# One core, a state-space recurrence and a long convolution: the recurrence taken at every second step, both stages woven into one planned order

## The chip, the cores and the metric

One core of one Trainium2 chip. The metric is the device time of one execution in microseconds (us). A profile is one execution of it, and its span is 1 to 2 us shorter than the time. A run counts as fast, slow or unknown by its clock and by how far it lies above the fastest of the same kernel (over 1.5% is slow); only fast runs are compared.

## The reference, cut to what matters

`x` is 2048 time steps by 1024 features. Two results are mixed by a gate: a diagonal complex recurrence (1024 states) and a causal convolution with filters as long as the sequence.

```python
def _A_ref(x, Lambda_re, Lambda_im, B_re, B_im, C_re, C_im, log_dt, Dskip):
    ...
    Lam_bar = jnp.exp(dt * Lam)
    Bu = jnp.einsum("bld,pd->blp", x + 0j, B_bar)
    for t in range(L):
        h = Lam_bar[None, :] * h + Bu[:, t, :]
        hs.append(h)
    y = 2.0 * jnp.einsum("blp,dp->bld", hseq, Cmat).real + x * Dskip[None, None, :]

def _B_ref(q, k, v, shift_k, ssm_k, ssm_D):
    for t in range(ks):                       # ks = 4
        k_shift = k_shift + k_pad[:, t:t + S, :] * shift_k[:, ks - 1 - t][None, None, :]
    kv = k_shift * v
    ...                                       # FFTs of kv and ssm_k, product, inverse FFT: y
    y = y + kv * ssm_D[None, None, :]
    return q * y

x = A_x
g = _sigmoid((x * gate_w).sum(-1, keepdims=True))
a = _A_ref(x, ...)
b = _B_ref(x, B_k, B_v, B_shift_k, B_ssm_k, B_ssm_D)     # q is x
return g * a + (1 - g) * b
```

## The kernel before

Two stages, one behind the other. The convolution is a Fourier transform in matmuls. It goes in 8 units of 128 channels. Every unit writes its shifted product to DRAM and reads it back in another layout (`kv_scr`), then goes through `stage1`, `spec`, `product`, `inverse`, a shuffle between partitions by DMA (`zb`) and `final`:

```python
def kv_steps(job):
    ...                                       # four taps on DVE
    nc.vector.tensor_tensor(out=acc, in0=acc, in1=vT, op=ALU.mult)
    nc.sync.dma_start(out=kv_scr[c0:c0 + 128, :], in_=acc)
...
for u in range(NU):
    ...
    for q in range(4):
        spec(z, kv, q, 0, "A")
        if u + 1 < NU:
            stage1(a, zs[u + 1], w, 2 * (q % 2), "V")
        spec(z, kv, q, 1, "A")
        pp_new = product(kv)
        ...
        if pend is not None:
            inverse(*pend, "A")
    if u + 2 < NU:
        va[u + 2] = load_A(kv_scr, u + 2, "va")
```

The recurrence turns the complex scan into two real ones: multiply by a rotating phase (tables `tbc`, `tbs`), scan with the real radius, turn back. It does this for each of 4 time blocks of 512 steps and each of 8 state tiles:

```python
for pi in range(NP):
    ...                                       # B.x: 16 matmuls of 512 columns, two copies on ACT
    nc.vector.tensor_tensor(out=t1, in0=tbc, in1=bure, op=ALU.mult)
    nc.vector.tensor_tensor(out=t2, in0=tbs, in1=buim, op=ALU.mult)
    nc.vector.tensor_tensor(out=pre_re, in0=t1, in1=t2, op=ALU.add)
    ...                                       # the same for pre_im
    nc.vector.tensor_tensor_scan(out=Wre, data0=rcol_bc, data1=pre_re, initial=init_re,
                                 op0=ALU.mult, op1=ALU.add)
    nc.vector.tensor_tensor_scan(out=Wim, data0=rcol_bc, data1=pre_im, initial=init_im,
                                 op0=ALU.mult, op1=ALU.add)
    ...                                       # six more DVE operations turn back: hb_re, hb_im
for tl in range(TT_B):
    ...                                       # C.h: 16 matmuls of 512 columns into psy
    nc.scalar.activation(out=ga, in_=psy, func=ACT.Identity, scale=gcols[:, tt_:tt_ + 1])
    nc.scalar.activation(out=m_t, in_=dsk[:, d0:d0 + DHW], func=ACT.Identity, scale=gcols[:, tt_:tt_ + 1])
    nc.scalar.activation(out=pbs, in_=pbb[:, d0:d0 + DHW], func=ACT.Identity, scale=omg[:, tt_:tt_ + 1])
    nc.vector.tensor_tensor(out=u_t, in0=m_t, in1=pbs, op=ALU.add)
    nc.vector.tensor_tensor(out=u_t, in0=u_t, in1=x_tt[:, d0:d0 + DHW], op=ALU.mult)
    nc.vector.tensor_tensor(out=ot[:, d0:d0 + DHW], in0=u_t, in1=ga, op=ALU.add)
```

## Time and profile before

| | before |
|---|---|
| time, median of 4 runs in the rounds with the changed kernel | 644.6 us (644.16 to 646.3) |
| span of the profile | 643.4 us |
| tables and first loads | 0 to 56 us |
| convolution | 56 to 296 us |
| preparation between the stages | 296 to 371 us |
| recurrence and output | 371 to 643 us |

The prediction below shows the lines that carry this table. First a window of the kernel before (stretch in us, its length, then busy us and count of PE, weight loads, DVE, ACT and GpSimd, then granted TensorE clock, share of the DMA engines, GB/s):

```profile
0.00:56.00 56.00, 3.59 (x16) 2.19 (x16) 36.06 (x82) 25.96 (x30) 4.10 (x10) 1.00 1.00 173
```

For its first 56 us PE has next to nothing to do (3.59 us), while the DMA engines are full (1.00). Then two groups and a queue from its page (a group: line, engine, operation, tiles, shapes, count, then busy us and ns of one, then idle before it):

```profile
L573 DVE TENSOR_TENSOR_SCAN Wre<-rv,init_re,pre_re 128x512 bf16<-128x512 f32 x24 | 30.6, 1276 | 0.0
...
L611 ACT ACTIVATE ga<-psy,gcols 128x512 bf16<-128x512 f32 x32 | 21.3, 676 | 38.6 <-PE psy L607 37.5
```

```profile
q1 hardware_dynamic: 157312, 54.54, 39.6%
```

A scan costs DVE 1.28 us and never waits (idle before it 0.0). The first operation of the epilogue stands behind the last output matmul. The main queue keeps the DMA engines busy for 39.6% of the span.

### The profile page before, as it was taken

The page shows a single profiled execution, that of the slowest core. Times are in us where ns is not written, and L with a number is a line of the kernel's source. Part 1 is how long each engine was busy: PE and PEld are TensorE (multiplying, and loading weights), DVE is VectorE, ACT ScalarE, POOL GpSimd, SP SyncE. Part 2 cuts the span into 40 slices and gives each one's busy share as a digit, 9 for nine tenths or more (in the row PEclk, how much of TensorE's full clock was granted, in tenths as well). Part 3 has the DMA queues.
Part 4 walks back from the last instruction along what each step waited for, and adds up shares of the span by engine and source line. Part 5 has one row for each costly group of instructions (what it writes and reads, how often), then busy time and mean ns, then how long its engine had stood idle before and what let it go on. Part 6 is the DMA issues. An engine that isn't in the chain of part 4 may idle for free.

```text
span 643.4 us, 6726 instructions
## 1 busy us (share of the span) xinstructions
PE 410.0 (64%) x2240; PEld 212.4 (33%) x2240; DVE 465.4 (72%) x1059; ACT 306.4 (48%) x415; POOL 4.1 (1%) x10
## 2 busy tenths in 40 slices
PE   0023877484747493953451087999699978998577
PEld 0011654252424362631110033344244433443133
DVE  7649997393939462630372389999999899989952
ACT  3832865454454664741369961264126611552042
POOL 2000000000000000000000000000000000000000
PEclk9999997778887888876875578999889998999579
DMA  9899705564749364135994022041204200110001
GB/s 173 154 163 254 164 26 131 120 143 100 162 84 175 70 131 89 43 98 103 169 201 116 17 83 59 7 131 66 63 4 130 83 0 1 52 64 0 2 16 49
DMA packets 166026, 59.44 MB, mean 92 GB/s; under 512 B 142312, under 2 KB 158696, under 8 KB 165992
## 3 DMA queue, kind: packets, MB, share of 16 engines
q1 hardware_dynamic: 157312, 54.54, 39.6%
q10 hardware_dynamic: 8680, 4.48, 2.8%
q8 instruction: 17, 0.28, 0.2%
q14 instruction: 17, 0.14, 0.1%
HBM read 17.06 MB, written 12.58 MB: 46 GB/s over the span
## 4 chain that ended last, share of the span: by engine, by line
DVE 41%; PE 21%; ACT 11%; DMA 9%; SPq 9%; issue 5%; ACTq 0%; DVEq 0%
DVE Wim L575 5%; DVE Wre L573 5%; DMA va<-kv_scr 4%; SPq L363 4%; PE ps L336 3%; ACT kv L285 3%; PE ps L327 3%; DVE acc L306 2%; PE psy L607 2%; PE psy L604 2%; PE ps L356 2%; SPq L491 2%; DVE pre_re L549 2%; DVE pre_im L555 2%; DVE hb_re L584 1%
## 5 line engine op out<-in xcount | busy, mean ns | idle before, releaser
L285 ACT CAST kv<-ps 128x1024 bf16<-128x1024 f32 x64 | 64.3, 1015 | 65.8 <-PE ps L338 58.3
L283 DVE CAST zkv<-ps 128x1024 bf16<-128x1024 f32 x28 | 34.2, 1220 | 50.0 <-PE ps L327 49.8
L327 PE MATMUL ps<-tab_188,va 128*128 128x256 bf16 x128 | 25.4, 341 | 57.5 <-DMA va<-kv_scr 55.7
L336 PE MATMUL ps<-zkv,fC 128*128 128x512 bf16 x128 | 54.7, 428 | 6.2 <-ACT kv L285 4.9
L604 PEld LDWEIGHTS <-hb_re 128*128 128x128 bf16 x256 | 25.7, 102 | 76.2 <-DVE hb_re L584 46.1
L285 ACT CAST qq<-ps 128x1024 bf16<-128x1024 f32 x32 | 32.5, 1019 | 32.1 <-DMA zb<-qq 29.6
L327 PE MATMUL ps<-tab_188,ka 128*128 128x256 bf16 x128 | 20.9, 295 | 42.0 <-DVE ka L321 41.4
L285 ACT CAST zkv<-ps 128x1024 bf16<-128x1024 f32 x36 | 36.1, 1022 | 22.1 <-PE ps L327 22.0
L607 PEld LDWEIGHTS <-hb_im 128*128 128x128 bf16 x256 | 26.1, 103 | 47.6 <-issue 18.4
L542 ACT ACTIVATE bure<-bu_re 128x512 bf16<-128x512 f32 x32 | 19.1, 597 | 47.3 <-PE bu_re L535 18.5
L613 ACT ACTIVATE m_t<-dsk,gcols 128x512 bf16<-128x512 bf16 x32 | 23.1, 723 | 35.6 <-DVE u_t L617 32.7
L611 ACT ACTIVATE ga<-psy,gcols 128x512 bf16<-128x512 f32 x32 | 21.3, 676 | 38.6 <-PE psy L607 37.5
L337 PE MATMUL ps<-zkv,fS 128*128 128x256 bf16 x128 | 38.4, 300 | 0.0
L338 PE MATMUL ps<-zkv,fN 128*128 128x256 bf16 x128 | 38.3, 299 | 0.0
L356 PE MATMUL ps<-pp,gC 128*128 128x256 bf16 x128 | 32.5, 288 | 8.6 <-ACT kv L285 5.0
L327 PEld LDWEIGHTS <-va 128*128 128x128 bf16 x128 | 14.9, 120 | 64.2 <-DMA va<-kv_scr 57.5
L374 PE MATMUL ps<-zb,tabFc 128*128 128x512 bf16 x32 | 15.1, 473 | 28.7 <-DMA zb<-qq 28.7
L573 DVE TENSOR_TENSOR_SCAN Wre<-rv,init_re,pre_re 128x512 bf16<-128x512 f32 x24 | 30.6, 1276 | 0.0
L575 DVE TENSOR_TENSOR_SCAN Wim<-rv,init_im,pre_im 128x512 bf16<-128x512 f32 x24 | 30.5, 1271 | 0.0
L543 ACT ACTIVATE buim<-bu_im 128x512 bf16<-128x512 f32 x32 | 19.1, 596 | 22.5 <-PE bu_im L538 22.5
L306 DVE TENSOR_TENSOR acc<-acc,tmpj 128x2047 bf16<-128x2047 bf16 (+2 forms) x24 | 29.3, 1222 | 0.5
L357 PE MATMUL ps<-pp,gN 128*128 128x128 bf16 x128 | 29.2, 228 | 0.0
(793 smaller groups left out, 1153.3 us busy)
## 6 DMA issues: line engine op xcount, KB each, us to landing
zb<-qq SPq DMA_DIRECT2D x128, 64.0 KB
ka<-in_B_ssm_k_dram SPq DMA_DIRECT2D x8, 512.0 KB
kv_scr<-acc SPq DMA_DIRECT2D x8, 512.0 KB
va<-kv_scr SPq DMA_DIRECT2D x8, 512.0 KB
pB_scr<-cv SPq DMA_DIRECT2D x16, 256.0 KB
out_dram<-ot SPq DMA_DIRECT2D x16, 256.0 KB
pbb<-pB_scr ACTq DMA_DIRECT2D x8, 256.0 KB
x_tt<-in_A_x_dram SPq DMA_DIRECT2D x8, 256.0 KB
```

Source lines behind the costliest of these rows:

```text
L283: nc.vector.tensor_copy(o, i_)
L285: nc.scalar.copy(o, i_)
L306: nc.vector.tensor_tensor(out=acc[:, j:S], in0=acc[:, j:S], in1=tmpj[:, 0:S - j], op=ALU.add)
L327: nc.tensor.matmul(ps[:, i, :], lhsT=a[:, 4 * q + i, :], rhs=t1v, start=True, stop=True)
L336: nc.tensor.matmul(ps[:, i], lhsT=fC[:, k2, :], rhs=z[:, k2], start=True, stop=False)
L337: nc.tensor.matmul(ps[:, i, :, 0, :], lhsT=fS[:, k2, :], rhs=z[:, k2, :, 1, :], start=False, stop=False)
L338: nc.tensor.matmul(ps[:, i, :, 1, :], lhsT=fN[:, k2, :], rhs=z[:, k2, :, 0, :], start=False, stop=True)
L356: nc.tensor.matmul(ps[:, i], lhsT=gC[:, k2, :], rhs=pp[:, i], start=True, stop=False)
L573: nc.vector.tensor_tensor_scan(out=Wre, data0=rcol_bc, data1=pre_re, initial=init_re, op0=ALU.mult, op1=ALU.add)
L575: nc.vector.tensor_tensor_scan(out=Wim, data0=rcol_bc, data1=pre_im, initial=init_im, op0=ALU.mult, op1=ALU.add)
L604: nc.tensor.matmul(psy, lhsT=hb_re[:, pi, tl * 128:(tl + 1) * 128], rhs=CTr[pi][:, d0:d0 + DHW], start=(cnt == 0), stop=(cnt == n_mm - 1))
L607: nc.tensor.matmul(psy, lhsT=hb_im[:, pi, tl * 128:(tl + 1) * 128], rhs=CTi[pi][:, d0:d0 + DHW], start=(cnt == 0), stop=(cnt == n_mm - 1))
```

## The change

**Intent.** (1) Let the scan run over even time steps only, and get the odd states from the even ones by diagonal matmuls on PE, so that DVE has half as many blocks. (2) Take the recurrence over all time, state tile by state tile. The output then needs all states at once, so half of them are spilled to DRAM and read back. (3) Spread the convolution units among the recurrence. (4) No pools and no dependence-driven scheduling: the builder lists every operation with an assumed duration and a priority, simulates the core and thereby fixes the order on each engine and the place of each buffer (21 slabs of 8 KB, 8 PSUM halves). (5) Smaller matters: fused epilogue, gates in four column strips of the array, some transfers issued from GpSimd, warm-up matmuls at the start.

The diff has some 1700 lines; this is its core, with cuts marked.

```diff
+class _Plan:
+    def op(self, eng, dur, fn, r=(), w=(), prio=0.0, dma=None, alt=None):
+        ...                                # records what it reads and writes
+    def schedule(self, free0):
+        ...                                # simulates: the ready operation of least priority number goes next
+                        cand = sorted((o for o in waiting[e] if o.ready <= now + 1e-9), key=lambda o: (o.prio, o.idx))
+                        ...
+                        if not take(o):    # no slab or PSUM half free
+                            continue
...
-                nc.vector.tensor_tensor(out=t1, in0=tbc, in1=bure, op=ALU.mult)
-                nc.vector.tensor_tensor(out=t2, in0=tbs, in1=buim, op=ALU.mult)
-                nc.vector.tensor_tensor(out=pre_re, in0=t1, in1=t2, op=ALU.add)
-                ...
+            def turn(out, x):
+                TT(out=out, in0=tab.ap.unsqueeze(2).to_broadcast([128, 2, 2, CW]),
+                   in1=x.unsqueeze(1).to_broadcast([128, 2, 2, CW]), op=ALU.mult)
+            def f():
+                turn(T.ap, ue())
+                TT(out=T.ap[:, 0, 0, :], in0=T.ap[:, 0, 0, :], in1=T.ap[:, 1, 1, :], op=ALU.add)
+                TT(out=T.ap[:, 0, 1, :], in0=T.ap[:, 0, 1, :], in1=T.ap[:, 1, 0, :], op=ALU.subtract)
+            op("DVE", 2.08, f, r=[(H, 0), tab], w=[T], prio=pr)
...
+        def odd(dg, Hc, pi, c, pr):
+            def f():
+                for ri in range(2):
+                    PE_.matmul(ps.ap[:, ri, :], lhsT=ident, rhs=Hc[c].ap[:, 1, ri, :], start=True, stop=False)
+                    for k in range(2):
+                        PE_.matmul(ps.ap[:, ri, :], lhsT=dg.ap[:, LMAT[ri][k], :], rhs=Hc[c].ap[:, 0, k, :],
+                                   start=False, stop=(k == 1))
+            op("PE", 6 * MM(512), f, r=[dg, Hc[c]], w=[ps], prio=pr)
+            evac(lambda: Hc[c].ap[:, 1], lambda: ps.ap, r=[ps], w=[(Hc[c], 1)], prio=pr)
+            if pi < NP - NKEEP:
+                dma(QB, 1.6, lambda: [h_scr[pi, c]], lambda: [Hc[c].ap.rearrange("p a b s -> p (a b s)")], [Hc[c]],
+                    [(e_h, (pi, c))], pr, alt=QA)
...
-                    nc.scalar.activation(out=ga, in_=psy, func=ACT.Identity, scale=gcols[:, tt_:tt_ + 1])
-                    ...
-                    nc.vector.tensor_tensor(out=ot[:, d0:d0 + DHW], in0=u_t, in1=ga, op=ALU.add)
+                op("DVE", 0.77, lambda: STT(out=ot.ap[:, ti, :], in0=ps.ap, scalar=col(gcols, gi[ti]),
+                                            in1=pb.ap[:, ti, :], op0=ALU.mult, op1=ALU.add),
+                   r=[ps, pb, e_gate], w=[(ot, ti)], prio=prs[ti])
...
+    sg = s5()
+    next(sg)
+    conv()
+    for _ in sg:
+        pass
+    order = pl.schedule({"DVE": 9.8, "ACT": 9.5, "PE": 4.6, "POOL": 3.0, "SP": 0.7})
+    with tc.manual_schedule():
+        pl.emit(order, slabs, psums)
```

## The prediction

> **What bounds the kernel now.** I read the page first, for the shape of the span in time:
>
> ```profile
> span 643.4 us, 6726 instructions
> PE 410.0 (64%) x2240; PEld 212.4 (33%) x2240; DVE 465.4 (72%) x1059; ACT 306.4 (48%) x415; POOL 4.1 (1%) x10
> ...
> PE   0023877484747493953451087999699978998577
> ...
> DVE  7649997393939462630372389999999899989952
> ...
> PEclk9999997778887888876875578999889998999579
> ```
>
> No engine is at its limit over the whole span, but the digits show two kernels one behind the other. In slices 1 to 18 (the convolution, 16 us a slice) PE and DVE take turns; in slices 24 to 38 (the recurrence) DVE stands at 8 and 9. Then the windows view with one window per stage (columns: busy us and count of PE, weight loads, DVE, ACT, POOL, then granted clock, DMA share, GB/s):
>
> ```profile
> 56.00:296.00 240.00, 152.51 (x1064) 102.47 (x1064) 153.82 (x249) 130.80 (x135) 0.00 (x0) 0.84 0.54 115
> 296.00:371.00 75.00, 23.20 (x76) 8.28 (x77) 28.26 (x60) 49.06 (x60) 0.00 (x0) 0.64 0.62 122
> 371.00:644.00 273.00, 230.70 (x1084) 99.47 (x1083) 247.28 (x669) 100.52 (x191) 0.00 (x0) 0.91 0.15 48
> ```
>
> Convolution: 240 us in which PE and DVE each have 153 us of work, so neither bounds it and about 87 us are waiting. Between the stages: 75 us where no engine is busy two thirds of the time, because tables, C and x are made ready only then. Recurrence: DVE busy 247 of 273 us, it is the bound there. The waits view says what is waited for in the convolution:
>
> ```profile
> ACT kv L285 <- PE ps L338: 58.3, 34, 7.2
> PEld L327 <- DMA va<-kv_scr: 57.5, 6, 13.5
> PE ps L327 <- DMA va<-kv_scr: 55.7, 6, 13.1
> DVE zkv L283 <- PE ps L327: 49.8, 11, 10.8
> ```
>
> The first stage of a unit stands behind a DRAM round trip (55.7 us in six waits); a single unit is in work, so nothing fills the hole. The chain of waits, in a part of the recurrence, shows DVE following itself:
>
> ```profile
> 432.02 1.19 DVE Wre L573
> 433.40 0.33 DVE r_t_3549 L582
> 433.73 1.19 DVE Wim L575
> 434.93 0.32 DVE ot L619
> ```
>
> A 128x512 product costs the chain 0.33 us and a scan 1.19 us (their recorded spans are 0.42 and 1.27: neighbours overlap). And the timeline gives the price of a matmul when nothing holds it up:
>
> ```profile
> 420.11 0.38 PE L607 MATMUL psy<-CiT_2588,hb_im 128*128 128x512 bf16 x1
> ...
> 420.32 0.38 PE L604 MATMUL psy<-CrT_2600,hb_re 128*128 128x512 bf16 x1
> ...
> 420.54 0.38 PE L607 MATMUL psy<-CiT_2602,hb_im 128*128 128x512 bf16 x1
> ```
>
> 0.215 us start to start, though each record lasts 0.38. At half clock it is 0.43 (the records at 310 us).
>
> **What the Trainium skill says.** "TensorE: Matmul & The Clock Gate", section "Wait — 56ns, not 53.3ns?": warm, back-to-back matmuls start N/2.4 ns + about 2.5 ns apart, 215.7 ns for 512 columns and 55.6 for 128. The trace agrees: 0.215 above, and 71.79 to 71.85 us for a 128-column one. Same page, "What's actually happening": after an idle window of about 3.4 us the clock falls to half and needs as long to recover. The granted clock of 0.84 and 0.64 where PE starves and 0.91 where it is dense fits. "VectorE: DVE Perf Modes", "Side-by-side: where the cycles go for N=2048 bf16": a two-source bf16 operation of 2048 elements takes 1224 ns; the trace has 1.22 us (acc on L306). "SBUF — State Buffer", "Who interferes with whom": a DVE instruction in a two-port mode and GpSimd exclude one another, and DMAs issued from GpSimd need that port for their descriptors. The kernel before issues none there, so its trace can't say.
>
> **The change part by part.**
>
> 1. *Recurrence decimated by two.* The scan runs over even time steps only; odd states come from even ones by a complex multiply with a diagonal, done as matmuls. Before, each of 32 blocks (8 state tiles x 4 time blocks) had 12 products or sums and 2 scans: 12 x 0.34 + 2 x 1.2 = 6.5 us, plus tiny carries, 0.9 us: 236 us. After, 16 blocks of 512 even steps, each with two 128x2048 products with a broadcast operand (1.2 each), four 128x512 sums (0.34) and two scans (1.2): 6.2 us, in all 99. DVE saves about 137 us. PE pays: 64 matmuls of 511 columns for the previous odd input (13.8 us) and 96 of 512 for the odd states (20.7), 34 us more.
> 2. *Epilogue.* Before, 3 sums on DVE and 3 ACT operations for each of 32 half tiles: 39 and 67 us. After, one fused DVE operation from PSUM (22 us; 0.7 us each is my estimate, a little over half of the 1.22 us of a 1024-wide PSUM read on DVE), 30 fused ones (21) and 15 products (10) ahead of it: 53 us on DVE, but only the 0.7 us lies behind the matmuls. ACT keeps 32 x 0.71 = 23.
> 3. *Convolution.* The same columns on PE: stage 1 now 512 matmuls of 128 columns, 28.6 us; spectrum 55.6; inverse 28.3; final 13.8. DVE: shift taps 61, products 32 x 1.2 + 64 x 0.34 = 60 (before 0.6 + 4 x 0.34 for each of 32, about 63), the final multiply by x moves into the PSUM read (16 x 1.22 = 20). Of the 28 + 8 evictions DVE had, 10 stay; ACT has 197 x 1.02 = 201 us of them.
> 4. *All else*: C scaling 18 us and tables 26 on DVE.
>
> Sums from the changed kernel's order of instructions and these prices: DVE 362 us by recorded spans (about 345 start to start), before 465. ACT 289, before 306. PE: B·x 110.6, previous 13.8, odd 20.7, convolution 126.3, output 110.5, gates 2 to 7 (four column strips, perhaps side by side), warm-up 6: 391 to 396 us with the array warm. For the kernel before the same sum is about 350. So PE becomes the engine with most work, and the whole question is how densely it is fed.
>
> 5. *Interleaving and a planned order.* This is the greatest part: it removes the two-kernels shape. The 87 us of holes, the 75 us between, and the recurrence's 42 us of idle PE (273 less 231) have other work to fill them. PE's order shows it: up to 277 us of its own work, B·x, odd states and convolution alternate every few microseconds; then output; the last 368 output matmuls (79 us) are one unbroken run.
> 6. *Added traffic*: spilled states 8 x 0.5 MB written and read, and x once more for the convolution's product, 16 x 0.25 MB: 12.4 MB on 59.4.
>
> **The end, from two sides.** PE side: the gates need all of x. Ahead of it lie about 5 MB of transposing loads; before, five of 0.5 MB issued from 34.1 to 47.4 us, 2.66 us each, so 10 x 2.66 + 3 = 30 us. By then PE can have done 18 us of real work. 384 (without warm-up) - 18 = 366 us remain: 396 us. From the last matmul to the end of the span took 4.5 us before: floor 400. DVE side: its first rotation needs x whole and one B·x more, about 40 us; 283 us of DVE work lie between it and the last rotation, 269 start to start: 309; odd matmul and eviction 3; behind the last odd state PE has 91.5 us of output left, and 4.5 of tail: 408. Both engines must be nearly perfect to meet at 400 to 408. I add 4% for the granted clock (0.93 to 0.98 in the dense windows from 400 to 600 us) and 4% for waits that a fixed order can't dodge, 15 us each: **430 us**.
>
> **The rivals.**
> - *DMA becomes the bound.* Before, 42.4% of 643 us is 273 us of all 16 engines. With 71.8 MB at the same efficiency it is 330 us, 77% of 430. For it: slices at 9 at the start, packets under 512 B are 142312 of 166026, and transposes queue on one in-order issuer. Against it: the added spill is in 4 KB rows, and it spreads over the whole span. If it bites, loads land late and a fixed order can't work around them: 455 to 490.
> - *GpSimd-issued transfers starve.* 84 of the 128 shuffles of the inverse go there, four per group, while DVE's taps run in a two-port mode. Those take about 23 us of DVE time in all, so I expect delays of under 1 us, with nine buffers to hide them: 0 to 15 us.
> - *Broadcast operands lose the fast DVE mode.* The innermost 512 stay contiguous, so I expect 1.2 us; at one element a cycle 63 instructions would take about 1.07 us more each: 67 us, DVE the bound, about 490.
> - *The plan holds.* If PE stays warm and order fits, 405 to 412.
> - *Serialisation eats all*, as an in-order issue queue did before (the shuffles' queue waited 95.5 us for ACT). Even if PE had only today's 64% density, 391/0.64 = 611: still faster.
>
> **Range and chances.** The floors put the low end at 408; DMA or order trouble of the size named puts the high end at 465. Slower would need a density below today's, so faster by over 2%: 0.97, within 2%: 0.02, slower: 0.01.
>
> **What would show it.** Right: PE busy over 85% of the span from 30 us, granted clock 0.93 or more, DVE busy near 360, ACT near 290, 128x2048 products at 1.2 us, no DVE idle of tens of microseconds. Wrong: PE idle released by DMA in total above 40 us (rival one), DMAs from GpSimd with long waits on DVE (rival two), L911 or L772 near 2.3 us (rival three), clock under 0.88 (my 4% too small), PE idle released by DVE (DVE is the bound, the sum of part 4 too small).

## The result, and the profile after

The changed kernel takes 430.31 us (median of 4 runs, 428.82 to 435.28; one of them slow) against 644.6. The ratio of the fast runs is 0.6667 (95% interval 0.6649 to 0.6685). Here and below, a ratio is the mean time of one kernel's fast runs over the mean of the other's of the same rounds, so it is not quite the ratio of the medians. The outputs agree with the reference.

The page of the changed kernel, the lines that answer to those of the kernel before:

```profile
span 427.0 us, 7194 instructions
...
PE 398.4 (93%) x2691; PEld 228.5 (54%) x2736; DVE 346.7 (81%) x513; ACT 267.8 (63%) x310; POOL 132.7 (31%) x172
...
PE   7598999999999789999969999899989999999996
...
DVE  4998999999979789989889989979696969724422
...
PEclk9999999999999999999998999999999999999999
...
q1 hardware_dynamic: 146120, 54.55, 69.8%
q0 software_dynamic: 7360, 16.85, 16.9%
```

The two-kernels shape is gone. PE stands at 9 in nearly all slices, DVE mostly at 8 and 9 in the first 25, and the clock at full. The DMA engines went from 42.4% to 87% of the span (69.8 and 16.9 and small change): 71.87 MB (before 59.44) now move in two thirds of the time.

Where 216.4 us of span went, in PE's own terms. The full-clock price of PE's instructions (the sum in the prediction) was about 350 us before and is about 391 after, both worked out from 0.215 us per 512 columns. What PE was busy beyond that (half clock, drains) fell from 60 us (410.0 less 350) to 7 (398.4 less 391). What it was idle fell from 233 us (643.4 less 410.0) to 29 (427.0 less 398.4). So: 41 us more work, 53 us less lost to the clock, 205 us less idle.

The windows of the changed kernel, cut where the gates can start and where the last odd state is made:

```profile
0.00:37.00 37.00, 28.26 (x219) 18.50 (x222) 31.00 (x74) 22.48 (x31) 32.55 (x28) 0.95 1.12 148
37.00:331.00 294.00, 278.65 (x2056) 168.67 (x2091) 262.96 (x360) 219.58 (x244) 100.11 (x144) 0.99 0.97 184
331.00:427.00 96.00, 91.53 (x417) 41.37 (x423) 52.78 (x80) 25.77 (x36) 0.00 (x0) 0.99 0.49 127
```

In the 294 us of the middle PE lacks 15.35 us, DVE 31 and ACT 74, and the DMA engines are at 0.97. No engine but PE is near its limit. Whether the transfers are is not shown by their share of 0.97: the share passes 1 in the first window (1.12), and nopoolq below moves the same 184 GB/s in this stretch at a share of 0.90. The end is output alone. Why the cut lies at 331, the view of the odd states' line says (first and last start at the end of the times):

```profile
L950 PE MATMUL ps<-slab,slab x62: 377/379/380, 54.4 to 330.9; 128*128 128x512 bf16 x62
```

From the last of these matmuls to the end are 96.1 us, which the prediction put at 91.5 and 4.5. The chain of waits of the changed kernel (start, us, what):

```profile
13.16 6.07 SPq L513
...
29.68 7.28 DMA slab<-in_A_x_dram
37.00 1.91 PE ps L964 x31
...
55.62 6.91 PE ps L882 x32
...
68.14 0.89 PE ps L747 x16
...
212.17 11.65 DMA slab<-in_B_ssm_k_dram
...
353.05 10.74 PE ps L1125 x49
```

One piece of x holds the issuing queue (SPq) for 6.07 us, the last is issued at 29.68 us and lands 7.28 us later; then the gates' 31 recorded matmuls take 1.91 us (32 of 512 columns one behind the other would be 6.9: the four strips run side by side). 32 matmuls of 512 columns in 6.91 us are 0.216 us each and 16 of 128 columns in 0.89 us are 0.056, full speed. From 343.94 us the chain is output matmuls alone. What PE waits for in the middle stretch, from the waits view of that window (us in total, times, longest):

```profile
PE ps L747 <- POOL slab L712: 6.2, 2, 3.5
PE ps L786 <- DVE slab L776: 1.7, 2, 1.4
PE ps L805 <- DMA slab<-slab: 1.6, 1, 1.6
```

L712 is a small addition on GpSimd to a filter tile just loaded (0.69 us in the worst place), and the chain shows the load ahead of it: 512 KB that took 11.65 us from issue to landing. So the longest hole of PE is a transfer with a GpSimd operation behind it. The rest is crumbs. Last, three groups whose duration the prediction guessed:

```profile
L1134 DVE SCALAR_TENSOR_TENSOR slab<-ps,gcols,slab 128x512 bf16<-128x512 f32 x32 | 23.6, 747 | 39.1 <-PE ps L1125 36.1
...
L911 DVE TENSOR_TENSOR slab<-slab,slab 128x2048 bf16<-128x2048 bf16 x31 | 37.7, 1217 | 3.5 <-PE ps L747 1.5
L772 DVE TENSOR_TENSOR slab<-slab 128x2048 bf16<-128x2048 bf16 x32 | 38.6, 1215 | 1.8 <-ACT slab L520 1.5
```

The broadcast products (L911, L772) take 1.22 us, the fused operation from PSUM (L1134) 0.75.

### The profile page after: what moved, and what is told of

Same layout as the page of the kernel before. It is cut to its first block, busy times and chain, and to the rows that moved or that the text cites. A ratio compares the mean times of both kernels' runs of the same rounds, so it can differ in the third digit from the quotient of the medians.

```text
span 427.0 us, 7194 instructions
## 1 busy us (share of the span) xinstructions
PE 398.4 (93%) x2691; PEld 228.5 (54%) x2736; DVE 346.7 (81%) x513; ACT 267.8 (63%) x310; POOL 132.7 (31%) x172
## 2 busy tenths in 40 slices
DMA packets 153596, 71.87 MB, mean 168 GB/s; under 512 B 129861, under 2 KB 147541, under 8 KB 153561
## 3 DMA queue, kind: packets, MB, share of 16 engines
q1 hardware_dynamic: 146120, 54.55, 69.8%
q0 software_dynamic: 7360, 16.85, 16.9%
HBM read 24.93 MB, written 16.79 MB: 98 GB/s over the span
## 4 chain that ended last, share of the span: by engine, by line
PE 68%; DMA 11%; SPq 10%; ACT 4%; DVE 3%; issue 3%; POOL 0%; DVEq 0%; ACTq 0%; POOLq 0%
PE ps L1125 22%; PE ps L882 20%; SPq L513 8%; DMA slab<-slab 5%; PE ps L760 4%; ACT slab L520 4%; PE ps L747 4%; DMA slab<-in_A_x_dram 4%; PE ps L889 3%; PE ps L950 3%; DMA slab<-in_B_ssm_k_dram 3%; PE ps L761 2%; PE ps L786 2%; PE ps L762 2%; SPq L515 2%
## 5 line engine op out<-in xcount | busy, mean ns | idle before, releaser
L520 ACT CAST slab<-ps 128x1024 bf16<-128x1024 f32 x197 | 185.4, 1042 | 62.8 <-PE ps L892 17.6
L882 PE MATMUL ps<-slab,slab 128*128 128x512 bf16 (+1 forms) x527 | 115.8, 370 | 6.3 <-DMA slab<-in_A_B_re_dram 3.1
L1125 PE MATMUL ps<-slab,slab 128*128 128x512 bf16 x485 | 109.1, 379 | 1.0 <-DVE slab L1134 0.4
L882 PEld LDWEIGHTS <-slab 128*128 128x128 bf16 x544 | 52.8, 99 | 60.0 <-issue 5.5
L1125 PEld LDWEIGHTS <-slab 128*128 128x128 bf16 x512 | 49.8, 98 | 59.6 <-issue 0.7
L515 POOL DMA_DIRECT2D slab<-slab x84 | 51.4, 618 | 57.8 <-ACT slab L520 51.9
L1134 DVE SCALAR_TENSOR_TENSOR slab<-ps,gcols,slab 128x512 bf16<-128x512 f32 x32 | 23.6, 747 | 39.1 <-PE ps L1125 36.1
L760 PE MATMUL ps<-slab,fC 128*128 128x512 bf16 x118 | 44.9, 381 | 1.1 <-ACT slab L520 0.6
L747 PE MATMUL ps<-tab,slab 128*128 128x128 bf16 x512 | 35.0, 222 | 7.5 <-POOL slab L712 6.2
L911 DVE TENSOR_TENSOR slab<-slab,slab 128x2048 bf16<-128x2048 bf16 x31 | 37.7, 1217 | 3.5 <-PE ps L747 1.5
L772 DVE TENSOR_TENSOR slab<-slab 128x2048 bf16<-128x2048 bf16 x32 | 38.6, 1215 | 1.8 <-ACT slab L520 1.5
L747 PEld LDWEIGHTS <-slab 128*128 128x128 bf16 x512 | 31.4, 99 | 12.3 <-POOL slab L712 6.8
L761 PE MATMUL ps<-slab,fS 128*128 128x256 bf16 x128 | 35.0, 273 | 0.6 <-issue 0.2
```

The source lines that it names most:

```text
L515: QS[q].dma_start(out=o_, in_=i_)
L520: op("ACT", 1.04, lambda: A.copy(o_(), i_()), r=r, w=w, prio=prio, alt=("DVE", 1.2, lambda: V.tensor_copy(o_(), i_())))
L747: PE_.matmul(ps.ap[:, i, :], lhsT=a.ap[:, 8 * q + i, :], rhs=t1v[:, hh * 128:(hh + 1) * 128], start=True, stop=True)
L760: PE_.matmul(ps.ap[:, i], lhsT=fC[:, k2, :], rhs=zz, start=True, stop=False)
L761: PE_.matmul(ps.ap[:, i, :, 0, :], lhsT=fS[:, k2, :], rhs=zz[:, :, 1, :], start=False, stop=False)
L772: TT(out=T.ap, in0=K.unsqueeze(2).to_broadcast([128, 2, 2, 4 * CH]), in1=W_.unsqueeze(1).to_broadcast([128, 2, 2, 4 * CH]), op=ALU.mult)
```

## The experiments

The prediction came true, so the question is whether for its reasons. The letters in the expectations stand for theories. A: the amount of PE work ahead of the last odd state sets the time. B: the fixed order with its small waits sets it, and every engine has slack that swallows part of any addition. C: transfers are at their limit. D: the second issuer, GpSimd, is needed. E: it is the searched order that brings PE to 93%. G: the gain is the two stages lying beside each other; G': it is the lighter DVE work. In dve18 and act17, B means that the loaded engine is itself a second bound, as the expectations say.

Twelve kernels ran: the first eight below on one chip, the last four on another. Each was compared with the kernel before on the same chip (medians 644.05 to 644.35). All twelve outputs passed the comparison with the reference; experiment 2 shows how little that vouches for.

### 1. pe20: 20 us more PE work, same order

```diff
                 for ri in range(2):
+                    for _ in range(3):
+                        PE_.matmul(ps.ap[:, ri, :], lhsT=ident, rhs=Hc[c].ap[:, 1, ri, :], start=True, stop=True)
                     PE_.matmul(ps.ap[:, ri, :], lhsT=ident, rhs=Hc[c].ap[:, 1, ri, :], start=True, stop=False)
```

> Same plan (order and buffers) as the changed kernel; each odd-state step issues its two identity matmuls of 512 columns three times more: 96 matmuls x 0.2158 = 20.7 us more on PE, result unchanged. Theory A (PE's work sets the time, 93% busy): +18 to +22 us, so about 449 to 453 against 430.3. Theory B (the engines wait on each other in turn and PE's density is incidental): less than half of it, +3 to +10 us, because part falls into PE's idle 28.6 us.

Measured: 443.12 us (442.45 to 445.4), ratio 0.6883 (0.6859 to 0.6907). Against the changed kernel (0.6667, and 0.6686 in a later control) that is 12.7 to 13.9 us. The busy line of this run's page and the line of its odd states:

```profile
PE 417.8 (95%) x2786; PEld 237.6 (54%) x2832; DVE 346.9 (79%) x513; ACT 268.4 (61%) x310; POOL 134.4 (31%) x172
```

```profile
L952 PE MATMUL ps<-slab,slab x61: 379/379/380, 53.8 to 345.0; 128*128 128x512 bf16 x61
```

PE has 19.4 us more, the last odd state comes 14.1 us later (345.0 against 330.9), and the tail behind it is the same (440.6 less 345.0 = 95.6). PE's idle time fell from 28.6 to 22.8: some 6 us went into holes. About 0.65 us per us of PE work: between the two theories, in the range of neither.

### 2. noident: 6.9 us less PE work, same order

This kernel leaves a term out and is mathematically wrong; the comparison does not see it at its tolerance, so that passing it vouches little for the recurrence, in the changed kernel too.

```diff
-                    PE_.matmul(ps.ap[:, ri, :], lhsT=ident, rhs=Hc[c].ap[:, 1, ri, :], start=True, stop=False)
                     for k in range(2):
                         PE_.matmul(ps.ap[:, ri, :], lhsT=dg.ap[:, LMAT[ri][k], :], rhs=Hc[c].ap[:, 0, k, :],
-                                   start=False, stop=(k == 1))
+                                   start=(k == 0), stop=(k == 1))
```

> Wrong result on purpose: the same plan with the identity matmuls left out (32 x 0.2158 = 6.9 us less on PE), nothing in their place. Theory A: -5 to -7 us, 423 to 425. Theory B: within 1.5 us of 430, the others' waits move into the hole.

Measured: fast runs 427.34, 429.08 and 431.41, ratio 0.6662 (0.6628 to 0.6695): no gain that could be told from none against 0.6667, about 1.5 us against the control. One run was slow (447.0) and the profile fell on it, so no trace of a fast run is at hand. Theory A misses here, B holds. Taking PE work away in this order buys little. That what PE waits for does not come sooner would explain it, but without a fast trace it is not shown.

### 3. dve18: 18 us more DVE work, same order

```diff
                 turn(U.ap, W.ap)
+                turn(U.ap, W.ap)
```

> Same plan; the second 128x2048 product of every rotation is done twice: 16 x 1.15 to 1.22 = 18.4 to 19.5 us more on DVE, result unchanged. Theory A: DVE (81% busy) has slack, but up to 300 us it is 90% busy and feeds PE, so +4 to +10 us. Theory B (DVE is a second bound up to the last rotation, as my floor of 408 us said): +14 to +19 us.

Measured: 433.87 us (430.95 to 434.19), ratio 0.6723 (0.6696 to 0.675): 2.4 to 3.6 us more.

```profile
PE 397.3 (93%) x2691; PEld 227.3 (53%) x2736; DVE 364.6 (85%) x529; ACT 268.4 (63%) x310; POOL 147.0 (34%) x172
```

This page shows DVE with 17.9 us more. About a fifth of that or less reaches the end, though all of it lies on the way to a state; the control's interval (0.6653 to 0.6718) even overlaps. That is less than either theory expected. DVE is not the bound.

### 4. act17: 17 us more ACT work, same order

Each odd state is copied out of PSUM twice.

```diff
-            evac(lambda: Hc[c].ap[:, 1], lambda: ps.ap, r=[ps], w=[(Hc[c], 1)], prio=pr)
+            op("ACT", 1.04, lambda: (A.copy(Hc[c].ap[:, 1], ps.ap), A.copy(Hc[c].ap[:, 1], ps.ap)), r=[ps], w=[(Hc[c], 1)], prio=pr,
+               alt=("DVE", 1.2, lambda: (V.tensor_copy(Hc[c].ap[:, 1], ps.ap), V.tensor_copy(Hc[c].ap[:, 1], ps.ap))))
```

> Same plan; the eviction of every odd state is done twice: 16 x 1.04 = 16.6 us more on ACT (a few on DVE), result unchanged. Theory A: ACT is 63% busy, +1 to +5 us, from the added latency only. Theory B: +8 to +16 us.

Measured: fast runs 432.04, 433.33 and 437.13, ratio 0.6738 (0.6697 to 0.6779): 3.4 to 4.6 us more (a fourth run, 440.09, was slow, and the profile fell on it). About a quarter of the addition, as theory A expected; here too the control's interval overlaps. ACT is not the bound either.

### 5. spill2: the spilled states written twice

```diff
+    h_scr2 = dram.tile([NP, NC, 128, 4 * CW], BF16, name="h_scr2")
...
-                dma(QB, 1.6, lambda: [h_scr[pi, c]], lambda: [Hc[c].ap.rearrange("p a b s -> p (a b s)")], [Hc[c]],
+                dma(QB, 1.6, lambda: [h_scr[pi, c], h_scr2[pi, c]], lambda: [Hc[c].ap.rearrange("p a b s -> p (a b s)")] * 2, [Hc[c]],
```

> Same plan; each of the eight spilled state blocks is written to DRAM twice: 8 x 0.5 MB = 4.2 MB more on 71.9 MB, 8 more issues, result unchanged. The queues' shares of the changed kernel's page add up to 87%, so 4.2 MB is about 22 us of all 16 engines. Theory C (transfers are a second bound, since the chain of waits goes through an 11.65 us filter load at 212 us and 69 us of other queue and DMA pieces): +8 to +20 us. Theory A (PE alone): +0 to +3 us.

Measured: 434.33, 441.13, 454.18 and 457.15 us. Only the first counts as fast, so there is no ratio: the size is inconclusive. The one fast run, the profiled one, is 4 us above the changed kernel's median.

```profile
HBM read 24.93 MB, written 20.98 MB: 106 GB/s over the span
```

This line of its page confirms the 4.2 MB (16.79 MB written without). The other three runs count as slow, and noident, which adds no transfer, also had a run 20 us above its fastest; so the spread can't be put down to the added transfers. Whether transfers are near their limit stays open here.

### 6. nopoolq: every transfer issued from one queue

Same order, same buffers; the transfers planned for GpSimd are issued by SyncE.

```diff
-    QS = {"SP": nc.sync, "POOL": nc.gpsimd}
+    QS = {"SP": nc.sync, "POOL": nc.sync}
```

> Same order of instructions; every transfer that GpSimd issues (84 shuffles and 33 others) is issued from the SP queue at its place in that order. Rival two of the prediction (transfers issued on GpSimd starve beside VectorE): faster by 3 to 12 us. Theory D (the second issuer is needed[...]): slower by 20 to 80 us.

Measured: 427.75 us (426.26 to 428.2), ratio 0.663 (0.6609 to 0.6652): 2.4 us faster than the changed kernel and 3.6 than the control, though the intervals just touch the changed kernel's. Theory D is refuted.

```profile
PE 401.0 (94%) x2691; PEld 229.0 (54%) x2736; DVE 345.6 (81%) x513; ACT 267.7 (63%) x310; POOL 62.2 (15%) x57
```

```profile
37.00:331.00 294.00, 282.15 (x2054) 169.91 (x2082) 265.96 (x366) 221.04 (x247) 32.73 (x32) 0.98 0.90 184
```

GpSimd's recorded time falls from 132.7 to 62.2 us; no other engine's busy time changes by more than 2.6. The middle stretch moves the same 184 GB/s at a share of 0.90 instead of 0.97. The Trainium skill, "DMA: Bandwidth & Descriptors", section "Issuing engines are not separate DMA queues", says that issuing on several engines only saves issue time, since the same 16 DMA engines do the work; this run agrees. For the prediction's GpSimd rival it gives a net figure: 2.4 to 3.6 us. A larger loss could hide only behind an equal cost of the single queue, which no run separates.

### 7. nowarm: 2 warm-up matmuls in place of 70

```diff
-            for _ in range(16):
+            for _ in range(1):
                 for j in range(2):
                     PE_.matmul(wps.ap[64 * j:64 * j + 64, 0, 0:128], ...)
-            for _ in range(6):
+            for _ in range(0):
...                                           (the two other groups likewise)
```

> Same plan; the 70 warm-up matmuls ahead of the first real one are cut to 2. If the granted clock of the first real matmuls depends on them: [...]PE waits for loads there in any case, so +0 to +2 us; the granted clock of the first 20 us falls from 0.98 to below 0.9.

Measured: 426.68 us (424.0 to 427.18), ratio 0.6613 (0.6588 to 0.6639): about 0.8% faster than the changed kernel. Its first window:

```profile
0.00:20.00 20.00, 14.08 (x92) 10.22 (x94) 14.46 (x45) 7.09 (x13) 16.44 (x20) 1.00 1.03 161
```

The column of the granted clock reads 1.00 in the first 20 us, not below 0.9 as I expected (from 20 to 40 us it was 0.91, against 0.93 with the warm-up). But that column does not show how the array starts. The first matmuls of B.x do, here and then in the changed kernel (ns least/median/most, first and last start):

```profile
L882 PE MATMUL ps<-slab,slab x32: 272/394/417, 9.1 to 14.3; 128*128 128x256 bf16 x32
L882 PE MATMUL ps<-slab,slab x32: 269/273/273, 10.0 to 15.7; 128*128 128x256 bf16 x32
```

Without the warm-up their median is 394 ns, with it 273. So the warm-up did speed them up; but PE then waited 2.1 and 3.1 us for loads all the same (two waits of L882 in the changed kernel), and the kernel without it was no slower. Why it was even 3.5 us faster is not shown.

### 8. order474: the same operations in a worse order

Only the priorities differ, shifted at random by a few units. The builder's own model takes this order for 47 us longer.

```diff
     PX = [95.0, 1.8]
+    PS = [[-423.74, -1082.05, 23.98, -789.47, -202.9, -1089.84, -331.87, -507.96, 64.56, -211.94, -1260.01], ...
...                                           (all other tables likewise; this row was -427.2, -1083.5, 24.9, -780.9 and so on)
```

> The same work (same matmuls, same transfers), with the priorities of the plan shifted at random by a few units; the builder lays out another order, which it believes to be 47 us longer. Theory E (the fixed order carries a large part of the gain): 465 to 485 us, PE busy the same 398 us, idle 70 us or more. Theory F (the engines' queues and semaphores smooth such differences out): 430 to 445 us.

Measured: 465.48 us (464.34 to 470.7), ratio 0.7239 (0.7196 to 0.7283): 36 us slower. Its windows and the longest waits of PE from 300 to 370 us:

```profile
0.00:300.00 300.00, 272.43 (x2037) 166.57 (x2071) 265.33 (x386) 221.66 (x250) 123.25 (x155) 0.98 1.01 177
300.00:370.00 70.00, 41.78 (x224) 22.20 (x225) 40.89 (x64) 34.03 (x43) 3.56 (x4) 0.76 0.66 135
370.00:468.00 98.00, 94.54 (x435) 42.99 (x441) 41.69 (x60) 14.67 (x22) 0.00 (x0) 1.00 0.30 94
```

```profile
PE ps L1132 <- DVE slab L1072: 12.3, 1, 12.3
PE ps L812 <- DMA slab<-in_A_x_dram: 8.1, 1, 8.1
PE ps L793 <- DVE slab L783: 6.4, 3, 4.7
```

Up to 300 us PE is nearly as dense as in the changed kernel (272.43 us busy against 277.60). Then come several holes. Output matmuls wait 12.3 us for a C tile that DVE has not scaled yet; DVE itself had waited 9.4 us for the load of that C, which was issued late. The last matmuls of the convolution wait 8.1 us, put down to a load of x, and 6.4 for DVE. The clock falls to 0.76, and 28 of 70 us are idle. Over the span PE is idle for 60.2 us (28.6 in the changed kernel) and busy for 408.7, where I expected 70 or more and the same 398. The busy time of DVE and ACT is the same to 3 us. So the order by itself is worth tens of us, and most of them are lost in a few late tiles near the end, not in a general thinning. Theory E holds.

### 9. seq: the same operations, convolution first

Added dependences keep the recurrence's loads, tables and B.x behind the last or last but one convolution unit, and the priorities were searched anew. The search had fewer tries than the author's, so the time may be a little too long. The load of the filter taps moves to the start of the kernel here and in experiment 10, since in the planned kernel three of the four taps declare no dependence on it; the original order meets it by its timing.

```diff
-                op("PE", 2 * ND * MM(CW), lambda: part(0, CW), r=[BT, (t, 0), (t, 1)], w=[ps], prio=pr)
+                op("PE", 2 * ND * MM(CW), lambda: part(0, CW), r=[(e_pB, (u, h)) for u in range(NU) for h in range(2)] + [BT, (t, 0), (t, 1)], w=[ps], prio=pr)
...                                           (likewise on the loads of B, x, C and the tables)
     sg = s5()
...                                           (conv() called ahead of it)
```

> Undoes the interleaving alone: the same operations as the changed kernel (decimated recurrence, fused epilogue), but B and x are loaded, the tables made and the recurrence's matmuls started only when the convolution has all but ended; its order is planned by the same builder with priorities of mine, searched for less long than the original's, so it is an upper bound of what that structure needs. Theory G (the interleaving carries most of the gain): 500 to 540 us, PE busy about 398 again and idle about 110. Theory H (the lighter work carries it): 430 to 460 us. The filter coefficients' tiny load is moved to the prologue here and in the next run, for a dependence that the original's plan meets by luck.

Measured: 516.58 us (514.83 to 521.76), ratio 0.8029 (0.7988 to 0.8069). The windows of this run and, from its timeline, the first matmul of the recurrence:

```profile
0.00:240.00 240.00, 160.61 (x1446) 119.23 (x1447) 171.11 (x263) 178.19 (x194) 52.16 (x78) 0.84 0.91 160
240.00:300.00 60.00, 50.18 (x282) 24.91 (x281) 34.69 (x58) 31.82 (x42) 6.18 (x8) 0.92 0.89 177
300.00:420.00 120.00, 120.00 (x584) 54.91 (x583) 98.33 (x132) 46.36 (x51) 17.03 (x27) 1.00 0.39 110
420.00:516.00 96.00, 92.12 (x427) 41.57 (x425) 45.09 (x70) 22.43 (x31) 0.00 (x0) 1.00 0.37 99
```

```profile
246.80 3.44 PE L890 MATMUL ps<-slab,slab 128*128 128x512 bf16 x8 [5.54 <-DMA slab<-in_A_B_re_dram]
```

By stages, against the kernel before: the convolution with all that precedes it ends at 241 us (before: 296), so 55 us less. PE then waits 5.5 us for B (before: 75 us of preparation, some of which, such as the scaling of C, now lies in the last stage), 70 us less. From there to the end are 269.5 us (516.3 less 246.8; before: 273). **In sequence the decimated recurrence is hardly shorter than the old one**: PE has 120.00 us of 120 between 300 and 420, so PE has taken DVE's place as the bound there, at nearly the same length. And the convolution alone leaves 79 us of PE holes in 240, at a clock of 0.84, with the transfers at 0.91. PE is busy for 422.9 us in all, not the 398 I expected, and idle for 93. Woven together (430) the kernel is 84 to 88 us faster than this (84 by the medians of the same chip, 87 to 88 by the ratios). Theory G expected this time; but 128 us come without any interleaving.

### 10. dve2: rotations and scans done twice, planned so

The interleaved order, with DVE's work of the recurrence doubled, as if it had not been decimated, and planned with those durations.

```diff
-            op("DVE", 2.08, f, r=[(H, 0), tab], w=[T], prio=pr)
+            op("DVE", 4.16, lambda: (f(), f()), r=[(H, 0), tab], w=[T], prio=pr)
...
-            op("DVE", 2.5, g, r=[T] + ([wl] if c else []), w=[W], prio=pr)
+            op("DVE", 5.0, lambda: (g(), g()), r=[T] + ([wl] if c else []), w=[W], prio=pr)
...
-            op("DVE", 2.08, h, r=[W, tab], w=[U, (H, 0)], prio=pr)
+            op("DVE", 4.16, lambda: (h(), h()), r=[W, tab], w=[U, (H, 0)], prio=pr)
...                                           (new priority tables; the taps' load as in experiment 9)
```

> Undoes the saving of the decimation on DVE alone: every rotation and scan is done twice (the same values again), planned with doubled durations: about 98 us more on DVE, near the price of the undecimated recurrence, while PE keeps its work. Theory G': with the convolution spread among it, DVE becomes the bound: 345 + 98 = 443 start to start before the last rotation's 97 us tail is counted, so 495 to 520 us. Theory H' (interleaving alone would do): 430 to 450.

Measured: 495.41 us (491.85 to 500.55, the last one slow), ratio 0.7671 (0.7647 to 0.7695).

```profile
PE 422.2 (86%) x2736; PEld 234.4 (47%) x2736; DVE 417.6 (85%) x600; ACT 332.3 (67%) x353; POOL 65.1 (13%) x75
```

This page has DVE at 417.6 (some copies went over to ACT, 332.3). DVE is busy for 340.7 of the 363.0 us up to the last odd state, and 130.5 us follow (96.1 in the changed kernel). The interleaved plan with all other changes, but without the lighter DVE work, is 149 us faster than the kernel before; the lighter DVE work then gives 63 to 65 more. That is an upper value, since the priorities were searched anew here too. The fourth kernel of this square, in sequence with the doubled DVE work, was not run.

### 11 and 12. best and after_ctl: a better version, and a control

`best` joins nopoolq and nowarm. `after_ctl` is the changed kernel with a comment added, as a control on the same chip.

```diff
-    QS = {"SP": nc.sync, "POOL": nc.gpsimd}
+    QS = {"SP": nc.sync, "POOL": nc.sync}
...
-            for _ in range(16):
+            for _ in range(1):
```

> The changed kernel with two parts taken out, same order otherwise: no warm-up matmuls (70 cut to 2) and no transfers issued from GpSimd. Each alone measured 2.5 to 3.6 us better. If both are real and independent: 422 to 425 us; if they were the luck of a chip or of one alignment of transfers: 426 to 430, same as the control.

> Control: the changed kernel unaltered (a comment added), on the same chip as the other three: 428 to 432 us, ratio 0.665 to 0.669.

Measured: best 426.5 us (425.07 to 428.51), ratio 0.6622 (0.6604 to 0.664). Control 432.69 us (427.08 to 437.88, six runs, one slow), ratio 0.6686 (0.6653 to 0.6718). The intervals just miss each other: the two edits together give about 1%, not more than either alone, in part by having no late runs (all four within 3.5 us).

```profile
PE 400.0 (94%) x2668; PEld 226.5 (54%) x2668; DVE 345.6 (82%) x513; ACT 267.2 (63%) x310; POOL 60.5 (14%) x57
```

PE is at 400.0 of a 423.3 us span. This version beats the changed kernel by a little.

## Why the prediction was right, and where its steps were not

**The number.** 430.0 was predicted and 430.3 measured, but not by the terms of the sum alone; errors cancelled. In the trace of the changed kernel PE's account reads: gates ready at 37.0 us; behind that 370.2 us of PE work (369.3 to the window's edge at 422.5, and 0.9); 3.6 us of tail; 16.2 us of holes; together 427.0. The prediction had 30, 366 and 4.5, and 30 us of allowance for clock and waits. So three terms changed it: the start +7, the work +4, the allowance −14. That they came out within 0.3 us is luck. (The span also leaves out 1.8 us of the time, which the sum did not price.)

**PE becomes the engine with most work, 391 to 396 us: right** (398.4 busy; the parts that the prediction lists add up to 1 us less than it says). DVE 345 to 362: right (346.7). ACT 289: 21 too high (267.8). The durations of the broadcast product, the fused operation and the scan, and the tail of 96 us, were right to a few per cent; the tail held in every fast profile that kept the order (95.5 to 97.4 us).

**The start, 30 us: wrong.** The step "10 x 2.66 + 3" has all the loads issued by 26.6 us and the last landed 3 us later. In the trace the last of them is only issued at 29.68 us and lands 7.28 us after that. So both terms were too small. The DMA share is over 1 in the first 40 us (1.08 and 1.19), tables and first units being loaded beside x; that this delays the pieces is likely, but was not tested.

**The clock, 4% = 15 us: wrong.** It was taken from windows of the kernel before in which PE still had gaps. The granted clock after is 0.99 (0.95 in the first 37 us), and PE's busy time exceeds the full-clock price by 7 us in all. In these runs the column was low where PE had gaps (0.64 and 0.84 before, 0.76 in the holes of order474), so for a dense PE the clock was no cost of its own.

**The waits, 15 us: right in size** (15.35 us in the middle stretch). The last rotation, which DVE's sum put at 309 us, came at about 326 and the last odd state at 330.9, so DVE was not back to back as that floor assumed.

**The rivals.** Transfers: share 87% where 77% was predicted (same megabytes, less efficiently moved than before). PE's waits behind them are about 8 us directly and 6.2 through the small GpSimd addition, far below the 40 us that would have made it the bound, but they are the largest single kind. How many us better transfers would give stays open, since spill2 was inconclusive. GpSimd: nopoolq puts it at 2.4 to 3.6 us net. Broadcast: no (1.22 us). Serialisation: a real danger, as order474 shows, but not for the order that was shipped.

**"Interleaving and a planned order ... the greatest part": this step failed in its mechanism.** The prediction did not part the two. It credited the holes of the convolution (87 us), the preparation (75) and the idle PE of the recurrence (42) to other work that fills them. Seq has a planned order but not that other work, and recovers 55 us up to the end of the convolution and 70 of the preparation: 128 us of the time with what the recurrence gives. At most 84 to 88 us of the 214 are interleaving, an upper value, as seq was searched less. How the 128 divide between the order, the early loads and the fused epilogue was not tested. And the gain of the decimation, 137 us of DVE work, is no term of its own: in sequence the recurrence with the output is 3 to 4 us shorter than before (269.5 against 273), interleaved the lighter DVE work gives 63 to 65. Neither is a clean measure: against the kernel before, the epilogue and the place of some preparation differ too. But in seq PE is busy for 261 of the last 269.5 us, so that a lighter DVE could not show there. The lighter DVE work pays where PE has other work to fall back on, and the two gains can't be added.

**What bounds it now.** Not one engine: an added us costs 0.65 on PE, about 0.25 on ACT, at most 0.2 on DVE, and a us taken from PE in this order gives little or nothing. PE's sum is the floor, and the 23 to 29 us above it are the late start, the tail and the waits of a fixed order. How the remaining holes split between transfers and latencies stays open.

## What to carry to other kernels

Price the work that a change takes from the bound engine against the engine that is next: the decimated recurrence was only 3 to 4 us shorter in sequence, where PE had become its bound, and the lighter DVE work was worth up to 64 once PE had something else to do. A stage boundary with 75 us of preparation shrank to a wait of 5.5 us when loads and tables started beside the last convolution units, before any further interleaving. With an order fixed in the builder, test its neighbours: a few units of priority cost 36 us here, most of it in a few holes behind late tiles.

## What the Trainium skill lacked or had wrong

- "TensorE: Matmul & The Clock Gate", section "Back-to-back issue gap", gives about 131 ns (512 columns) and 81 ns (128) for a long stream of matmuls with a weight load each, and calls the N/2.4 + 2.5 ns of the isolated gap too high and too low for it. Here each matmul of the streams of B.x and of the first transform has its own weight load, and they start 0.216 us apart (32 in 6.91 us) and 0.056 (16 of 128 columns in 0.89 us in the chain): the isolated formula, in a stream.
- The same page has the array start cold at half clock. This agrees (the first 32 matmuls of B.x with 256 columns: median 394 ns with 2 warm-up matmuls, 273 with 70), but the clock column of the profile read 1.00 in those first 20 us, a gap that the page, which calls such records unreliable, does not name. The time fell by 0.8% without the warm-up.
- "SBUF — State Buffer", section "Who interferes with whom", warns of transfers issued from GpSimd beside DVE's two-port modes, but not what it costs a kernel. Here taking all of them off GpSimd gave 2.4 to 3.6 us of 430, net.
- "DMA: Bandwidth & Descriptors" prices a single transfer, but not a load that shares the engines with many others: in a stretch with a share of 0.97 a 512 KB load took 11.65 us to land, and a piece of x 7.28 where the share was 1.12.
- "VectorE: DVE Perf Modes", the section on 2048 elements in bf16, gives 1224 ns for plain operands and does not speak of an operand repeated by broadcast over an outer dimension: here that costs the same, 1215 and 1217 ns.
